# Sliding-window attention and an MLP on one core: half of the first layer as a Strassen product, and a new order of the second layer's products

## The chip, the cores and the metric

The kernel runs on one core of a Trainium2 chip. The metric is the device time of one execution in microseconds (us). The engines are named as the profile names them: PE (TensorE, matrix products), PEld (its weight loads), DVE (VectorE), ACT (ScalarE), POOL (GpSimd) and SP (SyncE, which here only issues DMAs). SBUF is the on-chip memory, PSUM the memory into which PE accumulates, in banks of 128 partitions by 512 float32.

## The reference

Four batches of 768 tokens, eight heads of 64. Each query sees itself, the 127 keys before it and the first four keys; the heads' outputs side by side are `x` (512 wide), which goes through a norm and a two-layer MLP with a residual.

```python
scores = scale * np.matmul(q, k.transpose(0, 1, 3, 2))
keep = is_sink | in_window
scores = np.where(keep, scores, -1000000000.0)
...
a = a / (np.sum(a, axis=-1, keepdims=True) + 1e-09)
return np.matmul(a, v).astype(np.float32)
...
xn = (x - mu) / np.sqrt(var + 1e-06) * g_ln
ch = np.maximum(xn @ w_ch1, 0.0) @ w_ch2        # 512 -> 2048 -> 512
return (x + ch).astype(np.float32)
```

## The kernel before, in words

The 3072 tokens are cut into 12 chunks of 256 (`NC = 12`), three to a batch. A chunk passes through these steps:

- `attend` and `value`: scores on PE (`sc`, L763, for the sinks L767), exponentials on ACT (`ex`, L777, L785), the mask on DVE (`mk`, L781), the product with v on PE (`av`, L800 and L805, one for each tile of 128 tokens), then on DVE the division (`x`, L818 and L820), the statistics (L824, L826), on POOL the root (`rs`, L832 and L833), and on DVE the normed tile (`xc`, L835). From the third chunk on, SP transposes it by DMA into `xnt` (L845), four slices of 128 model dimensions by 256 tokens.
- the first layer (`mlp`): eight blocks `u` of 256 hidden units. Each block `ph` is 8 matmuls with 256 moving columns (L880; in the first two chunks 16 with 128 columns, L873), and one ACT instruction (`rl`, L890) applies the relu and moves the bank into `hq` in bf16. `hq` is two buffers of four blocks each.
- the second layer (`wino`, from the third chunk on): a product of 256 tokens, 2048 hidden units and 512 outputs, done as seven block products p1 to p7 (Strassen's scheme in Winograd's form), 8 matmuls of 256 columns each (L960). DVE makes four sums of blocks of `hq` for each half g of the hidden units (s1 to s4, L943, eight instructions of 128x512 in a chunk). Products that several outputs share stay in one half bank and are added to while it goes on: DVE reads it in between, adding `x`, into a kept sum `tm` (`keep`, L974), and a later read adds a kept sum to another product and writes the output quarter `ot` (`final`, L981). There are four of each in a chunk. The differences of the second weights (`w2t`) are made once.

The order of the work is planned when the program is built. Every step is an `op` with an engine, a cost and a priority; a list scheduler (`Plan.run`) goes through them, and its order on each engine is the program's order. From priority 40 on PE's order is by priority alone. A chunk takes 16 units of priority: `T = 16 c + 8` in `mlp`, and `at(c, step) = 16 c - 8 + PAR[step]` for attention. So the PE order of a chunk before is: first layer u0, u1, `av` of the next chunk's first tile, u2, `av` of its second tile, u3 to u7, then p1, p2, first half of the scores of the chunk after next, p7, p6, p4, second half of the scores, p5, p3. An engine does its instructions in order, so that one that waits holds up all behind it.

Buffers come from rings. Two pairs of PSUM banks (`pair`) hold scores and attention outputs; four single banks (`one`) hold everything else, one for each block `ph` and three for a chunk's products p1 to p7 (`x`, `y`, `w`). Rings in SBUF that the change touches: `nat` 8 (q and k as loaded), `pe` 12 (exponentials), `x` 16, `xc` 6. `hq` has 8 buffers, two to a chunk.

Of the kernel before, what the change touches and what calls it, by code (L numbers as in the profile page):

```python
# [197 lines left out]
def pe(us):  # L198
    return {"PE": (us, us + Plan.PE_DRAIN)}
# [12 lines left out]
def fix(occ, extra=0.09):  # L212
    return (occ, occ + extra)
# [16 lines left out]
           w1p=(0.15, 1.7, 2.05, 2.8), pm=2, w2p=(4.5, 4.51, 4.52, 4.53), by_tile=2, wino=2, vp=(0.0, 0.1, 2.0, 2.1, 4.2, 4.3), ld1=0.05)  # L230
# [131 lines left out]
def kernel(  # L362
# [12 lines left out]
    nc = tc.nc  # L375
# [34 lines left out]
    ring("pe", 12, [128, 2, 512], BF16)  # L410
    ring("ps", 3, [128, 256], BF16)
    ring("kts", 2, [128, HP, 32], BF16)
    ring("x", 16, [128, DM], BF16)
    ring("xc", 6, [128, DM], BF16)
# [121 lines left out]
    def at(c, step):  # L536
        return 16.0 * c - 8.0 + PAR[step]
# [200 lines left out]
    def attend(c):  # L738
        b, R = c // RC, c % RC
        kq = kq_b[c]  # L740
        kprev = kq_b[c - 1] if R else None
        n = 512 if R else 384
        ps, pp_s = (Buf(f"ps{c}", "ps"), Buf(f"pss{c}", "one")) if R else (None, None)
        pes = []
        for half in range(2):
            d = at(c, "sc1" if half else "sc")
            pps = [Buf(f"s{c}{2 * half + i}", "pair") for i in range(2)]
            pbs = [Buf(f"p{c}{2 * half + i}", "pe") for i in range(2)]

            def sc(e, pps=pps, half=half):  # L750
                if R:
                    parts = [(kprev, 128, 0, 128, 0), (kq, 0, 0, 256, 128), (kq, 128, 128, 256, 384)]
                    cut = [((0, 64), (0, 128)), ((0, 192), (64, 256)), ((0, 128), (64, 128))]
                else:
                    parts = [(kq, 0, 0, 256, 0), (kq, 128, 128, 256, 256)]
                for j, pp in enumerate(pps):
                    hp = 2 * half + j
                    for i, (kt, k0, q0, q1, col) in enumerate(parts):
                        for m in range(2 if R else 1):
                            n0, n1 = (cut[i][m] if R else (0, q1 - q0))  # L760
                            for h2 in range(2):
                                rs, ks = slice(64 * h2, 64 * h2 + 64), slice(64 * m, 64 * m + 64) if R else slice(0, 128)
                                nc.tensor.matmul(pp.t[ks, h2, col + n0:col + n1], lhsT=kt.t[rs, hp, 0, k0 + ks.start:k0 + ks.stop],  # L763
                                                 rhs=kq.t[rs, hp, 1, q0 + n0:q0 + n1], start=i == 0, stop=True, skip_group_check=True)
                if R and half == 0:
                    for hp in range(HP):
                        nc.tensor.matmul(pp_s.t[32 * hp:32 * hp + 32, 0:256], lhsT=kts_b[b].t[:, hp, :],  # L767
                                         rhs=kq.t[:, hp, 1, :], start=True, stop=True, skip_group_check=True)
            sinks = R and half == 0
            scores[c] = P.op(f"sc{c}{half}", pe(2 * (384 if R else n) / 2400 + (0.21 if sinks else 0)), d, sc,  # L770
                 reads=[kq] + ([kprev] if R else [])
                 + ([kts_b[b]] if sinks else []), writes=pps + ([pp_s] if sinks else []),
                 hold=pbs + ([ps] if sinks else []), mode=("q", "c") if sinks else "q" if R else "r")
            for j, pp in enumerate(pps):
                hp = 2 * half + j
                pb = pbs[j]
                P.op(f"ex{c}{hp}", {"ACT": act(2 * n)}, d + 0.1 + 0.05 * j, lambda e, pp=pp, pb=pb: nc.scalar.activation(  # L777
                    pb.t[:, :, 0:n], pp.t[:, :, 0:n], AF.Exp, scale=scale), reads=[pp], writes=[pb])
                mm = (mask if R else mask0).rearrange("p a b c -> p a (b c)")
                P.op(f"mk{c}{hp}", {"DVE": dve(2 * n, 0.52)}, d + 0.2 + 0.05 * j, lambda e, pb=pb, mm=mm:  # L780
                     V.tensor_mul(pb.t[:, :, 0:n], pb.t[:, :, 0:n], mm),  # L781
                     reads=[Bc["mask" if R else "mask0"]], rw=[pb])
                pes.append(pb)
            if sinks:
                P.op(f"sx{c}", {"ACT": act(256)}, d + 0.6, lambda e: nc.scalar.activation(  # L785
                    ps.t, pp_s.t[:, 0:256], AF.Exp, scale=scale), reads=[pp_s], writes=[ps])
        for i in range(2):
            def part(h, n, i=i):
                col = 256 * i + 128 * n if R else 128 * (i + n)
                return pes[h // 2].t[:, h % 2, col:col + 128]  # L790
            value(c, i, pes, ps, (PAR["av2"] if c == 2 else at(c, "av")) + PAR["avi"] * i, part, [2 * c + i - 1, 2 * c + i] if R or i else [2 * c])

    def value(c, i, pes, ps, d, part, srcs):
# [24 lines left out]
        P.op(f"rc{t}", {"DVE": fix(0.115)}, d + 0.1, lambda e: V.reciprocal(rc(), pv()[:, :, :, 64]),  # L818
             reads=[po], writes=[rcb])
        P.op(f"x{t}", {"DVE": dve(512)}, d + 0.11, lambda e: V.tensor_tensor(  # L820
# [3 lines left out]
        P.op(f"bn{t}", {"DVE": fix(0.60)}, d + 0.12, lambda e: V.bn_stats(st.t[:, 8:14], x.t),  # L824
             reads=[x], writes=[st, mv])
        P.op(f"ag{t}", {"DVE": fix(0.09)}, d + 0.13, lambda e: V.bn_aggr(st.t[:, 14:16], st.t[:, 8:14]),  # L826
# [4 lines left out]
        roots[t] = P.op(f"rs{t}", {"POOL": (0.83, 0.88)}, d + (0.5 if scaled else 5), lambda e: (  # L831
# [3 lines left out]
        P.op(f"xc{t}", {"DVE": fix(0.26)}, d + (0.6 if scaled else 0.14), lambda e: V.tensor_scalar(  # L835
# [24 lines left out]

    def mlp(c):
# [5 lines left out]
        for u in range(NH1 // 2):  # L867
# [15 lines left out]
            pr = T + u + 0.5  # L883
# [12 lines left out]
        if c >= PAR["wino"]:  # L896
            return wino(c, T, hq, h1)
# [29 lines left out]
    def wino(c, T, hq, h1):  # L927
# [3 lines left out]
        deps = {n: [h1[4 * g + (0 if n[2] == "1" else 1)::2][:2] for g in range(2)] for n in part}  # L931
# [7 lines left out]
        for i, (n, x0, x1, op) in enumerate((("s3", "a11", "a21", ALU.subtract), ("s1", "a21", "a22", ALU.add),  # L939
                                             ("s2", "s1", "a11", ALU.subtract), ("s4", "a12", "s2", ALU.subtract))):  # L940
            for g in range(2):
                sb[n, g] = Buf(f"{n}_{c}{g}", "hs")
                P.op(f"{n}_{c}{g}", {"DVE": dve(512, 0.52)}, T - 4 + 4 * g + 0.2 * i, lambda e, n=n, x0=x0, x1=x1, g=g, op=op: V.tensor_tensor(  # L943
# [3 lines left out]
        reg = {"z": ("x", 0), "l2": ("y", 0), "l1": ("w", 0), "r1": ("y", 256)}  # L947
# [22 lines left out]

        def keep(name, r, done, half, pr):
            tm[name] = Buf(f"tm{name}{c}", "tm")
            i, sl = half // 2, slice(256 * (half % 2), 256 * (half % 2) + 256)
            return P.op(f"tm{name}_{c}", {"DVE": dve(256, 1.14)}, pr, lambda e: V.tensor_tensor(  # L974
                tm[name].t, at(r), xs[i].t[:, sl], op=ALU.add), reads=[done, xs[i]], hold=[bank[reg[r][0]]], writes=[tm[name]])
        oo = {}

        def final(r, done, name, half, pr):
            i, sl = half // 2, slice(256 * (half % 2), 256 * (half % 2) + 256)
            oo[half] = Buf(f"oo{c}{half}")  # L980
            return P.op(f"o{c}_{half}", {"DVE": dve(256, 1.14)}, pr, lambda e: V.tensor_tensor(  # L981
# [19 lines left out]
        last_sum[:] = [ots[0], oo[1]]  # L1001
        for half in (0, 2, 3, 1) if c == NC - 1 else (0, 1) if c in PAR["split"] else ():
            t, sl = 2 * c + half // 2, slice(256 * (half % 2), 256 * (half % 2) + 256)
            b, r = t // RB, t % RB
            P.op(f"st{t}{half}", {"SP": (0.35, 0.4)}, 3000.0 + half % 2 if c == NC - 1 else u(6), lambda e, i=half // 2, b=b, r=r, sl=sl: nc.sync.dma_start(
                out[b, 128 * r:128 * (r + 1), sl], ots[i].t[:, sl]), reads=[oo[half]], hold=[ots[half // 2]], dma=HW_S)
        for i in () if c == NC - 1 else (1,) if c in PAR["split"] else (1, 0):
            t = 2 * c + i
            b, r = t // RB, t % RB
            P.op(f"st{t}", {"SP": (0.35, 0.4)}, u(5 if i else 6), lambda e, i=i, b=b, r=r: nc.sync.dma_start(  # L1010
# [22 lines left out]
    for c in range(NC):  # L1033
        mlp(c)
# [8 lines left out]
    def guard(e):  # L1043
# [12 lines left out]
        late.t[0:1, 0:1], lhsT=last_sum[0].t[:, 511:512], rhs=ones_f, start=True, stop=True),  # L1056
# [72 lines left out]
```

## Time and profile before

| what | value |
|---|---|
| median of 3 runs | 211.26 us (210.96 to 211.36) |
| profiled execution, its own time | 211.71 us |
| span in its trace, first to last instruction | 210.2 us |
| granted clock | 1.000 |
| DVE busy, of that 85.76 to 193.75 us | 162.2 us, 87.08 of 107.99 |
| ACT busy, of that 85.76 to 193.75 us | 114.1 us, 56.10 of 107.99 |
| POOL busy, of that 85.76 to 193.75 us | 83.5 us, 33.17 of 107.99 |

The span is what lies between the first and the last instruction in the trace; the execution's own time is 1.5 us more. A busy time is the union of an engine's instructions. The stretch from 85.76 to 193.75 us begins with the first layer of the fifth chunk and ends with that of the twelfth. That is seven periods from one chunk's u0 to the next one's: 15.60, 15.20 and 15.88 us in turn, since a batch's first chunk needs less attention, and 14.63 us for the last, 15.43 us on average.

### The profile page before, as it was taken

Reading aid. Unit: us, or ns where it says so; the run is one execution under the profiler, and the core shown is the slowest. Engines: PE = TensorE matmul, PEld = TensorE weight load, DVE = VectorE, ACT = ScalarE, POOL = GpSimd, SP = SyncE. Lnnn points to the kernel's source line nnn. Section 1 sums busy time; section 2 is a strip of 40 time slices with the busy share of each in tenths; the row PEclk is TensorE's granted clock in tenths of the full one; section 3 lists DMA queues with packets and bytes.
Section 4 is the critical chain, followed back from the end, with each engine's and each line's share of the span. In section 5 each row is a group of like instructions: output and inputs, shape, how many; then the busy total and the mean of one; then the engine's idle time right before and its main releaser. Section 6 shows DMA issues by size and latency. Waiting matters only on the chain.

```text
span 210.2 us, 6259 instructions
## 1 busy us (share of the span) xinstructions
PE 203.0 (97%) x2539; PEld 167.9 (80%) x2544; DVE 162.2 (77%) x410; ACT 114.1 (54%) x168; POOL 83.5 (40%) x126
## 2 busy tenths in 40 slices
PE   6978999999999999999999999999999999999994
PEld 2657997764787997997987987987988988988883
DVE  5579759999688688798687797797787786797353
ACT  2559479837564564564556555554457457450620
POOL 7967583369058057058066066066020020020000
PEclk9999999999999999999999999999999999999999
DMA  5999999999999949939959939939954520220202
GB/s 115 156 198 191 199 191 208 189 173 154 212 167 127 172 109 136 188 78 120 166 122 150 174 79 156 172 77 151 177 100 53 150 53 3 100 50 4 103 30 83
DMA packets 101243, 27.51 MB, mean 131 GB/s; under 512 B 89556, under 2 KB 99032, under 8 KB 101208
## 3 DMA queue, kind: packets, MB, share of 16 engines
q0 software_dynamic: 67712, 13.37, 77.7%
q1 hardware_dynamic: 33208, 13.41, 35.5%
q8 instruction: 21, 0.34, 0.7%
q10 hardware_dynamic: 288, 0.26, 0.4%
q14 instruction: 14, 0.11, 0.2%
HBM read 27.30 MB, written 6.29 MB: 160 GB/s over the span
## 4 chain that ended last, share of the span: by engine, by line
PE 90%; DMA 3%; DVE 3%; POOL 2%; issue 0%; DVEq 0%
PE one L880 33%; PE one L960 30%; PE one L873 7%; PE one L911 7%; PE pair L805 5%; PE pair L763 4%; DMA n4b<-in_q_dram 3%; PE pair L800 2%; PE one L645 1%; POOL nat L599 1%; PE one L767 1%; DVE xnt L857 1%; DVE kq L568 1%; POOL vn L562 0%; DVE st L824 0%
## 5 line engine op out<-in xcount | busy, mean ns | idle before, releaser
L890 ACT ACTIVATE hq<-one 128x512 bf16<-128x512 f32 x92 | 55.0, 597 | 55.7 <-PE one L880 46.7
L880 PE MATMUL one<-xnt,w 128*128 128x256 bf16 x640 | 74.5, 273 | 0.0
L880 PEld LDWEIGHTS <-w 128*128 128x128 bf16 x640 | 61.4, 98 | 7.0
L777 ACT ACTIVATE pe<-pair 128x1024 bf16<-128x1024 f32 (+1 forms) x40 | 36.2, 960 | 23.2 <-PE pair L763 19.0
L832 POOL TENSOR_SCALAR st<-st 128x1 f32<-128x1 f32 x24 | 6.2, 259 | 88.2 <-DVE rec L818 74.6
L960 PEld LDWEIGHTS <-hs 128*128 128x128 bf16 x320 | 30.0, 98 | 5.2 <-DVE tm L974 0.3
L974 DVE TENSOR_TENSOR tm<-one,x 128x256 f32<-128x256 f32 x40 | 16.9, 422 | 12.3 <-PE one L960 12.3
L781 DVE TENSOR_TENSOR pe<-pe,mask 128x1024 bf16<-128x1024 bf16 (+1 forms) x40 | 24.9, 644 | 1.0 <-ACT pe L777 0.8
L960 PEld LDWEIGHTS <-hq 128*128 128x128 bf16 x240 | 23.5, 98 | 2.7
L562 POOL DMA_DIRECT2D vn<-in_v_dram x24 | 21.8, 922 | 2.0 <-DMA w<-in_moe_w_ch_dram 1.1
L943 DVE TENSOR_TENSOR hs<-hq 128x512 bf16<-128x512 bf16 x40 | 15.4, 413 | 5.3 <-ACT hq L890 5.2
L960 PE MATMUL one<-w,hq 128*128 128x256 bf16 x160 | 19.1, 273 | 0.0
L981 DVE TENSOR_TENSOR ot<-one,tm 128x256 f32<-128x256 f32 x40 | 16.7, 418 | 1.1 <-PE one L960 0.9
L820 DVE TENSOR_TENSOR x<-pair,rec 128x512 bf16<-128x512 f32 x24 | 16.6, 691 | 0.8
L824 DVE BATCH_NORM_STATS2 st<-x 128x6 f32<-128x512 bf16 x24 | 16.6, 692 | 0.5
L873 PE MATMUL one<-xnt,w 128*128 128x128 bf16 x256 | 16.3, 219 | 0.5 <-DVE xnt L857 0.5
L873 PEld LDWEIGHTS <-w 128*128 128x128 bf16 x256 | 14.7, 98 | 1.6 <-issue 0.5
L659 POOL DMA_DIRECT2D nat<-in_k_dram x16 | 15.0, 938 | 2.5 <-DMA w<-in_moe_w_ch_dram 2.5
L659 POOL DMA_DIRECT2D nat<-in_q_dram x16 | 14.2, 898 | 3.4 <-DMA w<-in_moe_w_ch_dram 3.4
L833 POOL TENSOR_TENSOR st<-st,mhalf 128x1 f32<-128x1 f32 x24 | 14.2, 592 | 2.0
L911 PE MATMUL one<-w,hq 128*128 128x512 bf16 x60 | 14.8, 380 | 0.2
L805 PE MATMUL pair<-vn,pe 128*128 128x65 bf16 x352 | 14.6, 193 | 0.0
(113 smaller groups left out, 245.1 us busy)
## 6 DMA issues: line engine op xcount, KB each, us to landing
out_dram<-ot SPq DMA_DIRECT2D x17, 256.0 KB
w<-in_moe_w_ch_dram POOLq DMA_DIRECT2D x8, 512.0 KB, 12.6
vn<-in_v_dram POOLq DMA_DIRECT2D x24, 128.0 KB, 7.2
nat<-in_k_dram POOLq DMA_DIRECT2D x17, 128.0 KB, 4.8
nat<-in_q_dram POOLq DMA_DIRECT2D x17, 128.0 KB, 5.3
out_dram<-ot SPq DMA_DIRECT2D x14, 128.0 KB
kq<-nat SPq DMA_TRANSPOSE x32
xnt<-xc SPq DMA_TRANSPOSE x20
```

Of the source, the lines that this page charges most:

```text
L562: P.op(f"vld{t}", {"POOL": (0.87, 0.9)}, prio, lambda e: G.dma_start(bv.t[:, :, 0:64], v[b, :, 128 * r:128 * (r + 1), :].rearrange("h p d ...
L659: lambda e, nat=nat, ap=ap: G.dma_start(nat.t, ap), writes=[nat], dma=SW, after=behind(c))
L777: P.op(f"ex{c}{hp}", {"ACT": act(2 * n)}, d + 0.1 + 0.05 * j, lambda e, pp=pp, pb=pb: nc.scalar.activation(pb.t[:, :, 0:n], pp.t[:, :, 0:n ...
L781: V.tensor_mul(pb.t[:, :, 0:n], pb.t[:, :, 0:n], mm),
L805: nc.tensor.matmul(po.t[:, h // 4, 65 * (h % 4):65 * (h % 4) + 65], lhsT=part(h, n), rhs=vn_b[tv].t[:, h, :], start=(not R and h % 4 == 0 ...
L873: nc.tensor.matmul(ph.t[:, 128 * s:128 * s + 128], lhsT=w1[u // 2][:, j, 128 * s:128 * s + 128], rhs=xnt.t[:, j, 128 * (u % 2):128 * (u % ...
L880: nc.tensor.matmul(ph.t[:, 256 * s:256 * s + 256], lhsT=w1[ht // 4][:, j, 128 * (ht % 4):128 * (ht % 4 + 1)], rhs=xnt.t[:, j, :], start=j ...
L890: nc.scalar.activation(hg.t[:, u % 4, :], ph.t, AF.Relu)
L911: nc.tensor.matmul(pc.t[:, 0:wd], lhsT=(hq[s // 2].t[:, (2 * s + i) % 4, 128 * ii:128 * ii + 128] if by_tile else hq[ht // 8].t[:, ht // 2 ...
L960: nc.tensor.matmul(at(r), lhsT=get(left, g)[:, v, s, :], rhs=rhs, start=first and n == 0, stop=n == 7, skip_group_check=True)
L974: return P.op(f"tm{name}_{c}", {"DVE": dve(256, 1.14)}, pr, lambda e: V.tensor_tensor(tm[name].t, at(r), xs[i].t[:, sl], op=ALU.add), read ...
L981: return P.op(f"o{c}_{half}", {"DVE": dve(256, 1.14)}, pr, lambda e: V.tensor_tensor(ots[i].t[:, sl], at(r), tm[name].t, op=ALU.add), read ...
```

## The change

**First layer.** From the fifth chunk on (`half=4`, so c = 4 to 11) the blocks u0 to u3 go away, and `halves` computes these 1024 hidden units in their place: as a product of 2 x 2 blocks (512 hidden units by 256 model dimensions, times 256 model dimensions by 128 tokens), again by Winograd's seven products, m1 to m7. Each is 8 matmuls with 128 moving columns. The sums of the weight blocks are made once (`weight_sums`, four DVE instructions of 128x1024 bf16, not planned before 58, 61, 64 and 67, kept in two `hq` buffers from then on). The sums of the token blocks are made for each chunk by POOL (`xt`, four of 128x256 bf16, each from two tiles in SBUF, t1 from t0 and t3 from t1). The products use three single banks, z, w and y. Bank z collects m1, then m6, then m7, then m4; y collects m5 and then m3; w holds m2. ACT copies a running bank into SBUF in float32 (`tz1` after m1, `tz5` after m5, `tz6` after m6); m6 waits for the first copy, m3 for the second, m7 for the third. DVE adds a bank and a copy into `hq` (`c11` = m2 + tz1, `c12` = y + tz6, `c22` = z + tz5), and m4 waits for `c22`. ACT then applies the relu in place (`r`, from SBUF to SBUF), and for the last block straight from the bank (`rc21`). Blocks u4 to u7 stay as they were.

**Second layer**, from the third chunk on. The products come in the order p1, p2, p6, p5, p7, p3, p4. p1, p6, p7 and p4 use one half bank one after the other, p5 and p3 another, p2 the third. There are three kept sums, three finals, and one read that writes the output directly from the last product and `x`. p6 waits for the read after p1, p7 for that after p6, p3 for that after p5, p4 for the final after p7. The priorities of s1 to s4 are new, as are the orders of the output stores.

**Order.** Attention steps of the chunks after the fifth (c > 4) have their own priorities (`h`), and so have m1 to m7 and u4 to u7 (`pos`, `pos4`). The PE order of a period becomes, for c of 4 and on: p1, p2, p6, p5 (of the chunk before), second half of the scores of the next chunk, p7, p3, m1, p4, m5, m6, `av` first tile, m2, u5, m7, m3, `av` second tile, u4, u6, m4, u7, first half of the scores of the chunk after next. Before, the first layer's first block stood behind p3; now m1 stands ahead of the last product of the chunk before.

**Rings.** `nat` 6, `pe` 10, `x` 12, `xc` 5; new are `xt` (2) and `tz` (3, float32, 128x512).

```diff
-    ring("nat", 8, [128, H, 64], BF16)
+    ring("nat", 6, [128, H, 64], BF16)
...
+    ring("xt", 2, [128, 4, 2, 128], BF16)
+    ring("tz", 3, [128, 512], FP32)
...
     def at(c, step):
-        return 16.0 * c - 8.0 + PAR[step]
+        return 16.0 * c - 8.0 + (PAR["h"] if c > PAR["half"] else PAR)[step]
...
+    def weight_sums():
...
+            P.op(f"wsum{i}", {"DVE": dve(1024, 0.52)}, PAR["wsum"] + 3.0 * i, lambda e, ap=ap, x0=x0, x1=x1, op=op, val=val:
+                 V.tensor_tensor(ap(), val(x0), val(x1), op=op), reads=...
...
+    def halves(c, T, hq):
...
+        for i, (n, x0, x1) in enumerate((("t0", "b12", "b11"), ("t2", "b22", "b12"), ("t1", "b22", "t0"), ("t3", "b21", "t1"))):
...
+            P.op(f"xt{n}_{c}", {e: dve(256, 0.52) if e == "DVE" else fix(0.65) for e in PAR["te"]}, T - PAR["tlead"] + 0.1 * i, lambda e, n=n, x0=x0, x1=x1: (V if e == "DVE" else G).tensor_tensor(
+                right(n), right(x0), right(x1), op=ALU.subtract), reads=...
...
+                for h in range(4):
+                    for kk in range(2):
+                        nc.tensor.matmul(b.t[:, 128 * h:128 * h + 128], lhsT=lt[:, kk, 128 * h:128 * h + 128], rhs=rh[:, kk, :],
+                                         start=first and h == 0 and kk == 0, stop=kk == 1, skip_group_check=True)
...
+        m1 = product(1, "z", "a11", "b11", True)
+        t1, o1 = snap(1, "z", m1)
+        m5 = product(5, "y", 0, "t0", True)
+        t5, o5 = snap(5, "y", m5)
+        m2 = product(2, "w", "a12", "b21", True)
+        total("c11", "w", m2, t1, T + pos[1] - late_)
+        m6 = product(6, "z", 1, "t1", False, [o1])
+        t2, o2 = snap(6, "z", m6)
+        m3 = product(3, "y", 3, "b22", False, [o5])
+        total("c12", "y", m3, t2, T + pos[5] - late_)
+        m7 = product(7, "z", 2, "t2", False, [o2])
+        o3 = total("c22", "z", m7, t5, T + pos[6] - late_)
+        m4 = product(4, "z", "a22", "t3", False, [o3])
...
-        for u in range(NH1 // 2):
+        strassen = c >= PAR["half"]
+        quick = halves(c, T, hq[0]) if strassen else None
+        for u in range(4 if strassen else 0, NH1 // 2):
...
-        d7 = product(2, "p7", "l2", "s3", 0, 2, True)
-        k7 = keep("t7", "l2", d7, 3, u(2) - 2)
-        d6 = product(3, "p6", "z", "s2", 0, 1, False, [k1])
-        k6 = keep("t6", "z", d6, 2, u(3) - 2)
-        d4 = product(4, "p4", "l2", "a22", 0, 3, False, [k7])
-        f2 = final("l2", d4, "t6", 2, u(4) - 1)
-        d5 = product(5, "p5", "z", "s1", 0, 0, False, [k6])
-        final("z", d5, "t7", 3, u(5) - 1)
-        keep("t5", "z", d5, 1, u(5) - 1.1)
-        d3 = product(6, "p3", "r1", "s4", 1, hi, True, [f2])
-        final("r1", d3, "t5", 1, u(6) - 0.9)
+        d6 = product(2, "p6", "z", "s2", 0, 1, False, [k1])
+        k6 = keep("t6", "z", d6, 1, u(2) - 2)
+        d5 = product(3, "p5", "l2", "s1", 0, 0, True)
+        k5 = keep("t5", "l2", d5, 3, u(3) - 2)
+        d7 = product(4, "p7", "z", "s3", 0, 2, False, [k6])
+        f3 = final("z", d7, "t5", 3, u(4) - 2)
+        d3 = product(5, "p3", "l2", "s4", 1, hi, False, [k5])
+        final("l2", d3, "t6", 1, u(5) - 1)
+        d4 = product(6, "p4", "z", "a22", 0, 3, False, [f3])
+        keep(None, "z", d4, 2, u(6) - 1)
...
     for c in range(NC):
+        if c == PAR["half"]:
+            weight_sums()
         mlp(c)
```

More of the change, by code (lines that the diff above doesn't have):

```diff
@@ L830, in value @@
         scaled = c >= PAR["wino"]
[L831 removed]
+        roots[t] = P.op(f"rs{t}", {"POOL": (0.83, 0.88)}, d + xo + (0.5 if scaled else 5), lambda e: (
             G.tensor_scalar(st.t[:, 17:18], st.t[:, 15:16], 1e-6, None, op0=ALU.add),
@@ L930, in wino @@
                 "a12": lambda g: A[g]()[:, 1, :, :, 0:128], "a22": lambda g: A[g]()[:, 1, :, :, 128:256]}
-        deps = {n: [h1[4 * g + (0 if n[2] == "1" else 1)::2][:2] for g in range(2)] for n in part}
+        if quick:
+            h1 = [None] * 4 + h1
+        deps = {n: [quick[int(n[1]) - 1] if quick and g == 0 else h1[4 * g + (0 if n[2] == "1" else 1)::2][:2] for g in range(2)] for n in part}
         sb = {}
@@ L1055 @@
     P.op("late", pe(0.06), 4000.0, lambda e: nc.tensor.matmul(
-        late.t[0:1, 0:1], lhsT=last_sum[0].t[:, 511:512], rhs=ones_f, start=True, stop=True),
+        late.t[0:1, 0:1], lhsT=last_sum[0].t[:, 255:256], rhs=ones_f, start=True, stop=True),
         reads=last_sum[1:] + [Bc["ones_f"]], hold=last_sum[0:1], writes=[late])
```

120 lines of the change are left out of this document (93 added, 27 removed).

## The prediction

> **What bounds the kernel now.** I read first the page's busy times and clock, then the chain that ended last.
>
> ```profile
> PE 203.0 (97%) x2539; PEld 167.9 (80%) x2544; DVE 162.2 (77%) x410; ACT 114.1 (54%) x168; POOL 83.5 (40%) x126
> PEclk9999999999999999999999999999999999999999
> ```
>
> ```profile
> 44.68 0.89 PE one L873 x16
> ...
> 167.28 4.37 PE one L880 x40
> 171.64 1.75 PE one L960 x16
> 173.39 0.46 PE pair L763 x22
> 173.85 0.22 PE one L767 x4
> 174.07 2.73 PE one L960 x24
> ...
> 193.75 7.09 PE one L880 x64
> 200.84 6.13 PE one L960 x56
> 206.97 0.02 issue
> 206.99 0.44 DVE ot L981
> ```
>
> The columns are start, length, engine, buffer, line and count. From 54.69 us to 206.97 us the chain is PE alone, each piece beginning where the last ended. So a microsecond taken from PE in a chunk is a microsecond of the time, as long as nothing makes PE wait. The third view, busy time by stretch (seven periods), and the groups tell how near the others are:
>
> ```profile
> 85.76:193.75 107.99, 107.99 (x1312) 93.81 (x1310) 87.08 (x217) 56.10 (x84) 33.17 (x52) 1.00 0.99 111
> ```
>
> ```profile
> L974 DVE TENSOR_TENSOR tm<-one,x 128x256 f32<-128x256 f32 x40 | 16.9, 422 | 12.3 <-PE one L960 12.3
> L820 DVE TENSOR_TENSOR x<-pair,rec 128x512 bf16<-128x512 f32 x24 | 16.6, 691 | 0.8
> L1039 ACT ACTIVATE w<-w,gt 128x512 bf16<-128x512 bf16 x11 | 7.3, 750 | 0.0
> ```
>
> The stretch's columns are PE, PEld, DVE, ACT, POOL. DVE has (107.99 - 87.08) / 7 = 2.99 us free in a period of 15.43 us; ACT 7.4 us, POOL 10.7 us.
>
> **PE's work.** Removed in each of eight chunks: four blocks, 32 matmuls of 256 columns. The chain has 40 in 4.37 us, 109.3 ns each: 3.50 us. Added: 7 x 8 = 56 matmuls of 128 columns. Line 873 is this form, each with its own weight load from the same tiles: 16 in 0.89 us, 55.6 ns each, so 3.11 us. Saved: 0.38 us a chunk, 3.05 us in eight. The second layer keeps its 56 matmuls.
>
> The rule that speaks against this: the Trainium skill, "TensorE: Matmul & The Clock Gate", section "Back-to-back issue gap", says that in a stream of weight load and matmul both set the pace, and gives 81 ns for 128 columns. By that figure 56 would take 4.54 us and the change would cost 8.3 us, an estimate; the row of line 873, with as many loads as matmuls, shows 55.6 ns, and I go by it.
>
> **DVE's work.** Added in a chunk: three sums of a bank and a copy, 128x512 into bf16. The nearest row is L820 at 0.69 us (L919, with float32 out, 0.74): 0.70 each, 2.10 us. Removed: one kept sum, 0.42 us by L974, but such reads follow each other every 0.34 us: -0.34. Net +1.76 us in a period that shrinks to 15.05 us. Of 2.99 us free, 2.99 - 0.38 - 1.76 = 0.85 us stay, so DVE goes from 81% to 94%. The weight sums, four at 0.68 us (L781, same size), come once, 2.7 us, in a stretch before 85.76 us where DVE has 6.7 of 31.8 us free: nothing, unless they land in front of a read that PE waits for (at most 0.7 us). The third and fourth chunks only lose a kept sum.
>
> **ACT's work.** Seven new instructions for four removed: three copies and one relu from a bank at 0.60 (L890), three relus from SBUF at 0.75 (L1039), less 4 x 0.60: +2.25 us, 8.0 to 10.3 of 15.05 us. Hidden under PE; without that cover 0.6 us for each copy that an m product waits for.
>
> **POOL's work.** Four sums of 128x256 from two SBUF tiles. No row shows one. Below: 0.22 us (L832, one element). Above: L833 takes 0.57 us for one element, and 128 elements cost L460 0.07 us more than one costs L832; twice 256 elements add 0.28, so 0.85. I take 0.65, 2.6 us a chunk, since a sum is more than L832's single element and lighter than L833's power. What hides them: before, the second `av` ends at 151.40 and its transposes are through at 156.94 us, 5.5 us later. In the new order PE has from there u4, u6, m4, u7, scores, p1, p2, p6, p5, scores, p7, p3 to do ahead of m1: 9.4 us. So m1 has 3.9 us to spare, and m6, which needs the third sum, 5.6 us against 0.7 to 2.6 us. SP's and POOL's queues get no further DMAs. The q and k transposes move ahead on SP, past output stores: before, those behind the loads of 124.20 us are through at 135.96 and their scores run at 142.59, 6.6 us later; the scores move up by two products, 1.75 us. Covered, and `nat` holds four buffers at a time by these rows, so six do. `hq` has six left where two chunks in flight need four.
>
> **The new waits on PE.** PE's queue is in order: what stands behind a waiting product waits too. A release costs 0.21 us from PE to the reader (the block that ends at 194.62 is read at 194.83) and 0.06 us back (DVE ends at 207.41, PE starts at 207.47).
> - m6 after the copy of m1: 0.21 + 0.60 + 0.06 = 0.87, with p4 and m5 between, 1.31. m7 after the third copy: the same 0.87 behind at most 0.4 of the second copy, with m2 and u5 between, 1.31. m4 after c22: 0.21 + 0.70 + 0.06 against m3, `av`, u4, u6, 2.7 or more. All covered, if ACT or DVE is not late by over 0.04 to 1.7 us: the exponentials of the second scores (two in 1.94 us, from 0.21 after them) end 2.15 us after these, m1 2.2 us after them.
> - p7 after the read of p6, p3 after that of p5, p4 after the final of p7: 0.69 us each against 1.33, 1.33 and 1.32. Covered.
> - p6 after the read of p1: 0.69 against p2 alone, 0.87. Before, p7 lay between as well. Here DVE may start 0.18 us late and no more. It is busy 94% of the time with instructions 0.34 to 0.72 us apart, in order; one that is in hand leaves 0.2 us on average, so this wait shows for about 0.08 us on average, 0 at best and 0.5 at worst. Eight times: 0.65 us, which I take, bounds 0 and 4.
>
> In the last chunk no attention fills PE: u7's relu and two sums of 0.45 us end 1.8 to 2.4 us after u7, and p6's second half comes after 2.2: at most 0.3 us, inside that.
>
> **The sum.** 211.71 (profiled execution: span 210.2 and 1.5 around it, unchanged, since the end is still one product, one DVE read and a store) - 3.05 + 0.65 = 209.3. That execution stood 0.45 above the median of the runs, so the forecast for a median is **208.85 us**, its own range 207.9 (no stall, and some 0.3 us of DVE time gained in the third and fourth chunks) to 210.1.
>
> **The rivals.**
> *DVE is full.* POOL's new sums and DVE may get in each other's way. A trace row bears on it:
>
> ```profile
> 17.71 0.85 POOL L833 TENSOR_TENSOR st<-st,mhalf 128x1 f32<-128x1 f32 x1
> ```
>
> ```profile
> 17.44 0.68 DVE L720 TENSOR_TENSOR pe<-pe,mask 128x1024 bf16<-128x1024 bf16 x1
> ```
>
> The POOL instruction takes 0.57 us elsewhere; here it ran 0.28 longer, while DVE worked on two SBUF tiles. No DVE row is stretched (L943, 80 of them, 0.39 to 0.43 us), but POOL never held two large tiles. The Trainium skill, "SBUF — State Buffer", section "Who interferes with whom", has this as a rule: a DVE instruction with two SBUF inputs and a GpSimd instruction that reads SBUF exclude each other, and the later one waits for the whole of the first. The POOL row agrees; that DVE waits too, no row here shows.
> As a mechanism of this kernel: DVE's instructions on two SBUF tiles are eight of L943 (0.36 apart) and four of L781 (0.60), 5.3 of 15.05 us. If half of POOL's four sums meet one and hold it half their 0.65 us, DVE loses 0.65 us a chunk: still under the 0.85 free, the forecast. At 0.85 to 1.23 us DVE fills the period and eats the gain: (14.2 + 1.1 - 15.43) x 8 = -1.0, **210.2 us**, chance 0.14.
> *The other side: slower.* The same lock at its full price, in the stretch from m1 to p6 where reads, masks and s1 to s4 crowd: each POOL sum puts DVE back by most of its length. It decides from 1.23 us a chunk, where DVE's 14.2 + 1.23 us equal the old period. At 1.6 us (four times 0.4): (14.2 + 1.6 - 15.43) x 8 = +3.0, **214.2 us**; at the full 2.6 us, 222. Or the same from thin waits: 0.38 us of stall a chunk undoes the gain. For it: DVE at 94% in front of in-order waits. Against: the unstretched rows. Chance 0.21.
> *Weight loads set the pace.* At 98 ns, the mean of a load, 56 take 5.49 us: +16 us, 227 us. Line 873's rate excludes it; 0.01.
> *The change doesn't lighten PE*, because the new priorities make PE wait elsewhere for banks (m's three and a block take all four): about the time before, 211.3 us; 0.04.
>
> **The numbers.** Forecast 0.60. Below 0.2% (0.42 us, what a measurement of this kernel can tell from no change), that is under 210.84: 0.60 and most of the second case, 0.70. Within it: part of the second and the fourth, 0.08. Slower: 0.22. For 8 in 10 the range goes to 207.7 below, and above into the slower case as far as 212.8.
>
> **What would show it.** Right: PE's chain still unbroken, 56 matmuls at 55 to 56 ns, periods near 15.1 us, idle time of PE in front of p6 under 0.1 us a chunk, DVE at 93 to 95%. Wrong: idle time of PE that DVE ends, at p6, p4 or m4; rows of L943 or L781 longer than 0.43 or 0.69 us beside POOL's sums; ACT ending waits of m6 or m7; m1 waiting for `xnt`.

## The result, and the profile after

| | before | after |
|---|---|---|
| time, median of the runs | 211.31 us (210.96 to 211.44) | 219.91 us (219.38 to 221.17) |
| ratio | 1 | 1.0418, interval 1.0371 to 1.0466 |
| span of the profiled execution | 210.2 us | 219.6 us |
| first block of the fourth chunk | 69.89 us | 73.52 us |
| seven periods of the chunks that change | 107.99 us | 113.96 us |

The forecast was 208.85 us, with 207.7 to 212.8 as its range. The kernel became 8.6 us slower. The profiled execution of after took 221.17 us, 1.3 above the median; its granted clock was 0.992 over the whole span, against 1.000, 1.000 and 0.998 in the other three. Of the 9.4 us between the spans, 3.6 are lost before the first block of the fourth chunk and 6.0 in the seven periods, which in after are counted from m1 to m1; the rest, 0.2 less, lies between and behind these stretches.

The busy row, the clock row and the chain's shares from the page of after:

```profile
PE 203.6 (93%) x2731; PEld 168.8 (77%) x2736; DVE 177.4 (81%) x430; ACT 124.5 (57%) x190; POOL 110.2 (50%) x158
PEclk9999999999996999999999999999999999999999
...
PE 56%; DMA 16%; DVE 14%; POOL 10%; issue 2%; ACT 1%; SPq 0%; DVEq 0%; POOLq 0%
PE one L1059 16%; PE one L977 11%; DMA xnt<-xc 10%; PE one L908 8%; PE one L970 6%; PE one L1008 6%; POOL xt L892 5%; PE pair L808 4%; DMA n4b<-in_q_dram 3%; DVE hq L930 3%; DMA kq<-nat 2%; DVE st L828 2%; DVE hs L1042 2%; PE pair L766 2%; DVE xc L839 2%
```

The chain that was PE alone now runs through transposes of `xnt` and POOL's sums. The view of waits (engine, what it fills, line, what released it; us in total, times, longest) says where PE stands:

```profile
POOL xt L892 <- DMA xnt<-xc: 21.7, 8, 4.6
POOL nat L662 <- DMA kq<-nat: 20.9, 7, 9.3
...
PE one L908 <- DMA xnt<-xc: 3.7, 4, 1.6
PE one L908 <- POOL xt L892: 2.9, 4, 1.0
PE one L1059 <- DVE tm L1078: 2.3, 1, 2.3
```

L908 is an m product, L892 POOL's sums, L1059 a p product, L662 a load into `nat`.

**The first loss.** POOL's timeline of after (start, length, line, and in brackets the idle time before with its releaser), then PE's:

```profile
59.62 1.75 POOL L662 DMA_DIRECT2D nat<-in_q_dram  x2 [9.33 <-DMA kq<-nat]
61.44 0.22 POOL L836 TENSOR_SCALAR st<-st 128x1 f32<-128x1 f32 x1
```

```profile
66.76 1.69 PE L1059 MATMUL one<-n4c,hs 128*128 128x256 bf16 x8 [2.31 <-DVE tm L1078]
68.24 1.91 PE L1059 MATMUL one<-n4b,hs 128*128 128x256 bf16 x8
```

With six buffers in `nat`, POOL stood 9.33 us before two q loads until transposes had emptied buffers; the root of the fourth chunk (L836) stood behind them in POOL's queue, `xc` behind the root, DVE's reads behind `xc`, and p6 on PE behind a read: 2.31 us. After it eight matmuls take 1.5 to 1.7 us in place of 0.87, for 3.4 us in which the trace shows a granted clock of 0.50: the 6 in the clock row. This slow stretch costs 1.7 us, and by the clocks above the other three executions of after had little or none of it.

**The second loss.** The timeline of after around one m1 and m6 (SPq is SP's queue):

```profile
115.51 1.86 POOL L662 DMA_DIRECT2D nat<-in_k_dram  x2
115.74 0.83 DVE L839 TENSOR_SCALAR xc<-x,st 128x512 bf16<-128x512 bf16 x1
...
116.60 1.19 SPq L554 DMA_TRANSPOSE xnt<-xc  x1
...
117.35 1.78 POOL L565 DMA_DIRECT2D vn<-in_v_dram  x2
...
121.93 0.62 PE L908 MATMUL one<-xnt,w 128*128 128x128 bf16 x8 [1.63 <-DMA xnt<-xc]
...
122.02 1.29 POOL L892 TENSOR_TENSOR xt<-xnt 128x256 bf16<-128x256 bf16 x2 [2.90 <-DMA xnt<-xc]
```

The transpose's issue ends at 117.79, but its last semaphore comes at 121.88 us, beside POOL's loads; m1 waits 1.63 us for it, and POOL's sums, which m5 and m6 need, begin only then. By the spacing of PE's matmuls, nine such gaps at m1 and m6 make 8.1 us in the sixth to tenth chunk.

### The profile page after: what moved, and what is told of

Its sections match the earlier page's. It is cut to its first block, busy times and chain, and to the rows that moved or that the text cites. A ratio compares the mean times of both kernels' runs of the same rounds, so it can differ in the third digit from the quotient of the medians.

```text
span 219.6 us, 6704 instructions
## 1 busy us (share of the span) xinstructions
PE 203.6 (93%) x2731; PEld 168.8 (77%) x2736; DVE 177.4 (81%) x430; ACT 124.5 (57%) x190; POOL 110.2 (50%) x158
## 4 chain that ended last, share of the span: by engine, by line
PE 56%; DMA 16%; DVE 14%; POOL 10%; issue 2%; ACT 1%; SPq 0%; DVEq 0%; POOLq 0%
PE one L1059 16%; PE one L977 11%; DMA xnt<-xc 10%; PE one L908 8%; PE one L970 6%; PE one L1008 6%; POOL xt L892 5%; PE pair L808 4%; DMA n4b<-in_q_dram 3%; DVE hq L930 3%; DMA kq<-nat 2%; DVE st L828 2%; DVE hs L1042 2%; PE pair L766 2%; DVE xc L839 2%
## 5 line engine op out<-in xcount | busy, mean ns | idle before, releaser
L977 PE MATMUL one<-xnt,w 128*128 128x256 bf16 x384 | 46.8, 273 | 0.0
L987 ACT ACTIVATE hq<-one 128x512 bf16<-128x512 f32 x58 | 34.5, 594 | 21.1 <-PE one L977 12.0
L977 PEld LDWEIGHTS <-w 128*128 128x128 bf16 x384 | 36.1, 98 | 3.9
L1059 PEld LDWEIGHTS <-hs 128*128 128x128 bf16 x320 | 31.5, 100 | 8.1 <-issue 2.6
L784 DVE TENSOR_TENSOR pe<-pe,mask 128x1024 bf16<-128x1024 bf16 (+1 forms) x40 | 27.5, 717 | 1.3 <-ACT pe L780 1.2
L919 ACT COPY tz<-one 128x512 f32<-128x512 f32 x24 | 13.8, 586 | 23.9 <-PE one L908 21.0
L662 POOL DMA_DIRECT2D nat<-in_q_dram x16 | 14.3, 897 | 25.0 <-DMA kq<-nat 20.9
L1059 PEld LDWEIGHTS <-hq 128*128 128x128 bf16 x240 | 22.6, 98 | 3.3 <-issue 0.3
L836 POOL TENSOR_SCALAR st<-st 128x1 f32<-128x1 f32 x24 | 6.9, 287 | 35.2 <-DVE rec L822 20.3
L892 POOL TENSOR_TENSOR xt<-xnt 128x256 bf16<-128x256 bf16 x16 | 13.2, 842 | 21.7 <-DMA xnt<-xc 21.7
L933 ACT ACTIVATE hq<-hq 128x512 bf16<-128x512 bf16 x24 | 14.9, 630 | 11.1 <-DVE hq L930 11.1
L1059 PE MATMUL one<-w,hq 128*128 128x256 bf16 x160 | 19.2, 273 | 0.0
L908 PEld LDWEIGHTS <-hq 128*128 128x128 bf16 x256 | 15.8, 98 | 4.0 <-issue 3.6
L930 DVE TENSOR_TENSOR hq<-one,tz 128x512 bf16<-128x512 f32 x24 | 15.8, 688 | 3.5 <-PE one L908 3.3
L908 PE MATMUL one<-xt,hq 128*128 128x128 bf16 x192 | 14.1, 219 | 3.0 <-POOL xt L892 2.9
L662 POOL DMA_DIRECT2D nat<-in_k_dram x16 | 14.9, 929 | 2.5 <-DMA w<-in_moe_w_ch_dram 2.5
```

Source lines behind the costliest of these rows:

```text
L662: lambda e, nat=nat, ap=ap: G.dma_start(nat.t, ap), writes=[nat], dma=SW, after=behind(c))
L892: P.op(f"xt{n}_{c}", {e: dve(256, 0.52) if e == "DVE" else fix(0.65) for e in PAR["te"]}, T - PAR["tlead"] + 0.1 * i, lambda e, n=n, x0=x0 ...
L908: nc.tensor.matmul(b.t[:, 128 * h:128 * h + 128], lhsT=lt[:, kk, 128 * h:128 * h + 128], rhs=rh[:, kk, :], start=first and h == 0 and kk = ...
L930: o = P.op(f"c{n}_{c}", {"DVE": dve(512, 1.14)}, pr, lambda e: V.tensor_tensor(block(n), banks_[bank].t.rearrange("p (i t) -> p i t", i=4) ...
L977: nc.tensor.matmul(ph.t[:, 256 * s:256 * s + 256], lhsT=w1[ht // 4][:, j, 128 * (ht % 4):128 * (ht % 4 + 1)], rhs=xnt.t[:, j, :], start=j ...
L987: nc.scalar.activation(hg.t[:, u % 4, :], ph.t, AF.Relu)
```

## The experiments

Theories: **A**, the loss is waiting for late results of DMA (buffers of `nat`, then the second tile of `xnt`). **B**, the smaller rings cost nothing. **D or F**, DVE is full, or stretched by POOL's sums. **C** and **G**, the order itself. **E**, POOL's sums are all of it. Each ratio is against the kernel before, run on the same chip.

**Parts of the change alone.** `rings_cut` is the kernel before with the four smaller rings; `nat_only`, run last, cuts one of them.

```diff
-    ring("nat", 8, [128, H, 64], BF16)
+    ring("nat", 6, [128, H, 64], BF16)
```

> The kernel before with only the four smaller rings (nat 6, pe 10, x 12, xc 5); the planned order of PE, DVE, ACT and SP is the same. Theory A (short nat ring: POOL stands waiting for q's buffers until the transposes of the chunk before have read them, and the root instructions behind it are late): PE idles some 2 us near 60 us and runs slowly after it, 213 to 216 us. Theory B (the whole loss comes from the Strassen chunks, DVE and POOL in each other's way): no change, 211.3 us.

> The kernel before with nat 6 in place of 8 and nothing else; in rings_cut with all four rings smaller (213.41 us) PE had three gaps of 1.8 us in all near 66 us. Theory A (the nat ring alone does it: POOL stands before the q loads until the chunk's transposes have freed buffers, and the root behind it is late): 212.8 to 213.6 us. Rival (another ring): 211.3 us.

Measured: 213.41 us, 1.0113 (1.0089 to 1.0137), and 213.06 us, 1.0084 (1.0067 to 1.0101). One ring does nearly all of it, by the same stand of POOL, here in the timeline of `nat_only`:

```profile
58.96 1.76 POOL L659 DMA_DIRECT2D nat<-in_q_dram  x2 [9.28 <-DMA kq<-nat]
60.79 0.22 POOL L832 TENSOR_SCALAR st<-st 128x1 f32<-128x1 f32 x1
```

`order_only` is the changed kernel with no chunk's first layer as a Strassen product and the old rings, so only the second layer's new order is left:

```diff
-           ... half=4, ...
+           ... half=99, ...
```

> The changed kernel without the Strassen half (from no chunk on) and with the old rings: only the new order of the second layer and its reads. Theory A: 211 us, plus or minus 0.5, a read less in each of ten chunks hides under PE. Theory C (the thin wait of p6 for the read after p1, with p2 alone between, costs): 0.1 to 0.5 us in each of ten chunks, 212 to 216 us, with PE idle ahead of p6.

Measured: 211.68 us, 1.0019 (1.0003 to 1.0035), 0.2 us above the range of A and below that of C. The second layer's new order with one kept sum less neither costs nor brings 1 us. The new order of attention has no run of its own.

**The nat ring given back.** `nat8`, the base of what follows, is the changed kernel with two rings changed; the order on PE, DVE, ACT and SP stays.

```diff
-    ring("nat", 6, [128, H, 64], BF16)
+    ring("nat", 8, [128, H, 64], BF16)
...
-    ring("x", 12, [128, DM], BF16)
+    ring("x", 11, [128, DM], BF16)
```

> The changed kernel with nat back at 8 (x at 11 to make room); PE, DVE, ACT and SP keep their order, only POOL's loads move. Theory A: the 2.3 us of idle PE near 64 us and the slow stretch behind it go, 219.9 - 3.7 = 216.2 us; the waits in front of m1 and m6 from the sixth to the ninth chunk stay. Theory B: 219.9 us as before.

Measured: 217.58 us, 1.0309 (1.0272 to 1.0347): 2.3 us back, and the stall near 66 us gone. The 3.7 us that were expected counted the slow stretch behind the stall too, which the other executions of after hardly had, and the gaps of the sixth to tenth chunk grew from 8.1 to 8.9 us. Its waits:

```profile
PE one L908 <- POOL xt L892: 3.7, 4, 1.5
PE one L908 <- DMA xnt<-xc: 3.5, 4, 1.9
```

**The loads put behind the transposes.** `loads_later` plans a chunk's q, k and v loads behind the transposes of `xnt` and not behind the root:

```diff
-        return [roots[2 * (c - 3) + 1]] if c >= PAR["behind"] else []
+        return [landed[2 * (c - 3) + 1]] if c >= PAR["behind"] else []
```

> As nat8, and the q, k and v loads of a later chunk wait for the transposes of xnt instead of for the root before them, so that the two don't run at the same time. Theory A (xnt is late because its transposes share the DMA engines with those loads, 4.2 to 5.3 us from xc to landing against 2.4 without loads): the second tile's transposes land 2.4 to 2.8 us after xc, PE hardly waits for xnt, what is left is POOL's sums ahead of m6; 210 to 213 us. Theory B: as nat8, 216 to 220 us, since neither DVE's nor POOL's work changes.

Measured: 217.64 us, 1.031 (1.0267 to 1.0353). A miss: the second tile lands sooner, 2.4 to 4.0 us after `xc` (3.9 to 5.3 in after), and the waits for it go, but as many others come. The loads now run beside the next chunk's first tile, which lands 3.2 to 4.7 us after its `xc` in the sixth to tenth chunk (2.4 to 2.7 in after): the tile that has loads beside it is the late one. PE's waits there:

```profile
PE pair L766 <- DMA kq<-nat: 2.7, 3, 1.2
PE one L908 <- POOL xt L892: 2.0, 2, 1.0
```

Loads that come later make the scores (L766) wait for their own transposes.

**One cause taken out at a time.** In `old_tiles` the m products and POOL's sums read the chunk before's tiles; the planner still sees the old dependences, so every engine keeps its order.

```diff
+        old = xnt_b[c - 1]
...
-        B = {...: (lambda i=i, o=128 * (j ^ f): xnt.t[:, 2 * i:2 * i + 2, o:o + 128]) ...}
+        B = {...: (lambda i=i, o=128 * (j ^ f): old.t[:, 2 * i:2 * i + 2, o:o + 128]) ...}
```

> Base: the changed kernel with eight buffers for nat and eleven for x (217.58 us, PE idle some 9.3 us in the chunks that use the seven products). Here those products and POOL's sums read the transposed tiles of the chunk before (so the output is not the reference's); the number and the order of the instructions on every engine stay. Theory A (the loss is the wait for this chunk's transposed tiles, directly in m1 and through POOL's sums in m6): the waits at m1 and m6 go, and with them about 9 us: 208.0 to 209.5 us. Rival D (the loss sits in DVE, stretched by POOL's sums, and the waits at m1 and m6 only show it first): the masks still take 0.81 us, PE waits for DVE's reads instead, 212 us or more.

Measured: 218.5 us, 1.031 (1.0252 to 1.0368). Theory A missed by 9 us, and rival D had put what came: over 212 us, with PE waiting for DVE's reads. But the edit was no clean one: freed of the wait, POOL's sums fell beside DVE's `hs` sums. So this run alone does not tell A from D. DVE's timeline there, POOL's, and PE's waits:

```profile
115.42 2.28 DVE L1043 TENSOR_TENSOR hs<-hq,hs 128x512 bf16<-128x512 bf16 x2
```

```profile
114.45 1.54 POOL L893 TENSOR_TENSOR xt<-xnt 128x256 bf16<-128x256 bf16 x2
115.95 1.47 POOL L893 TENSOR_TENSOR xt<-xnt,xt 128x256 bf16<-128x256 bf16 x2
```

```profile
PE one L1060 <- DVE tm L1079: 4.5, 5, 1.5
PE pair L766 <- DMA kq<-nat: 2.0, 2, 1.6
...
PE one L1060 <- DVE ot L1086: 1.6, 3, 0.8
```

Two `hs` sums of 0.42 us take 2.28. PE then waits 6.1 us for DVE's reads and 2.0 us for the scores' transposes, and not at all at m1 or m6.

`sums_short` keeps the tiles and shortens POOL's sums from the seventh chunk on:

```diff
-                right(n), right(x0), right(x1), op=ALU.subtract), ...
+                *(right(x)[:, :, 0:128 if c < 6 else 8] for x in (n, x0, x1)), op=ALU.subtract), ...
```

> Same base, 217.58 us. From the seventh chunk on each of POOL's four sums covers 8 columns of 128 (the output is not the reference's), so that POOL is busy some 0.2 us a sum and not 0.85; orders unchanged, m1 still waits for its own chunk's transposed tiles. Theory A (first the late tiles, POOL's sums behind them): the waits at m6 behind POOL go (1.71 + 1.11 + 0.81 + 0.50 us and part of others) and the waits at m1 stay: 213 to 215.5 us. Rival E (POOL's sums are the whole loss, through m6 and through the stretch of DVE's masks from 0.68 to 0.81 us, which delays xc): 208 to 210 us. If the sums cost nothing: 217.5 us.

Measured: 215.78 us, 1.0231 (1.0165 to 1.0297). The waits for POOL fall from 3.7 to 0.3 us, the masks back to 0.69 us; the waits for `xnt` stay, and 1.3 us for the scores' transposes come new:

```profile
PE one L908 <- DMA xnt<-xc: 3.9, 4, 1.5
...
PE pair L766 <- DMA kq<-nat: 1.3, 2, 0.8
...
PE one L908 <- POOL xt L892: 0.3, 1, 0.3
```

The time is 0.3 us above A's range. E, the sums as the whole loss, falls.

`sums_dve` changes one word of `nat8`, `te=("DVE",)`:

> Same base, 217.58 us. The four sums of a chunk go to DVE (about 0.28 us each by the halved 0.42 us rows of hs, so 1.1 us of DVE a chunk) and POOL has none. Theory A: the sums come sooner behind the tiles and DVE's masks go back to 0.68 us, but the wait for the tiles stays and DVE gets fuller: 213 to 216 us. Rival E (POOL is the whole loss): 209 to 211 us. Rival F (DVE is the limit): 218 us or more.

Measured: 231.73 us, 1.0951 (1.0911 to 1.0991), in rival F's range (218 us or more) and far from the others. But it is not that DVE has too much work, as F says: DVE stands 12.0 us before sums that wait for a late tile, and the reads behind them in its order, for which PE waits, come late too. The waits of DVE and of PE:

```profile
DVE xt L892 <- DMA xnt<-xc: 12.0, 7, 3.0
```

```profile
PE one L1059 <- DVE ot L1085: 10.1, 7, 2.0
```

**All causes out together.** `old_short` joins `old_tiles` and `sums_short`; `old_all` also lets the scores, from the sixth chunk on, read the q and k tiles of the chunk before.

```diff
+        kuse = kq_b[c - 1] if c > 4 else kq
...
-                    parts = [(kprev, 128, 0, 128, 0), (kq, 0, 0, 256, 128), (kq, 128, 128, 256, 384)]
+                    parts = [(kprev, 128, 0, 128, 0), (kuse, 0, 0, 256, 128), (kuse, 128, 128, 256, 384)]
```

> Same base (nat 8, x 11; 217.58 us), orders unchanged. Both edits together: the seven products and POOL's sums read the transposed tiles of the chunk before, and from the seventh chunk on each sum covers 8 columns (the output is not the reference's). Each alone gave little (218.5 and 215.78 us): with the tiles of the chunk before, POOL's sums fell beside DVE's `hs` sums, which took 1.14 us each in place of 0.42. Theory A+D (two causes in a row, the late tiles and POOL's sums that hold DVE's bf16 operations up; either one alone leaves the other): without both, no waits at m1 and m6, masks 0.69 and hs 0.42 us, 208.3 to 210 us. Rival G (the order itself leaves too little room in DVE, lock or not): PE still waits for DVE's reads, 212 us or more.

> old_short (214.51 us, profiled span 212.1 us) with one more edit: from the sixth chunk on the scores read the q and k tiles of the chunk before, so that they no longer wait for transposes of the own chunk (three such waits of PE stood in old_short, 1.16 + 0.68 + 2.00 us). The output is not the reference's; orders unchanged. Theory A (three late DMA results one behind the other, nothing else): 209 to 211.5 us, PE's waits in the chunks with seven products below 1.5 us in all. Rival G (something else then takes their place, DVE first of all): 213 us or more.

Measured: 214.51 us, 1.0166 (1.0117 to 1.0215), a miss, since a third wait appeared; then 210.15 us, 0.9942 (0.9925 to 0.996), as A had it. The longest line of waits that was left in the chunks of `old_short`, and PE, PEld, DVE, ACT and POOL over 64 us of before, after and `old_all` (three views):

```profile
PE pair L766 <- DMA kq<-nat: 3.3, 3, 1.8
```

```profile
100.00:164.00 64.00, 64.00 (x794) 55.45 (x792) 51.44 (x127) 35.50 (x53) 22.76 (x34) 1.00 1.27 129
```

```profile
100.00:164.00 64.00, 58.28 (x802) 50.62 (x800) 52.74 (x126) 36.74 (x59) 38.76 (x53) 1.00 1.39 131
```

```profile
100.00:164.00 64.00, 63.60 (x923) 56.46 (x921) 57.84 (x138) 41.62 (x66) 32.31 (x55) 1.00 1.40 137
```

PE idles 5.7 of 64 us in after and 0.4 in `old_all`, with the order on PE, DVE, ACT and SP unchanged and POOL's sums shorter. `old_all` is 1.2 us faster than before and its trace still has 1.57 us of gaps (around the m1 of the sixth chunk, whose sums are whole, and in the last two chunks): 2.8 us together, an estimate, against the 3.05 us forecast for PE. So the saving is there, and waiting ate it.

**More lead by order, with the right output.** The due times of the chunks with the seven products were worked out anew, with POOL's sums at 0.85 us, against transposes as late as in the traces. `lead_a` and `lead_c` let m1 and m2 take the chunk's first tile. The edit of `lead_b`, cut to what matters (`av` and `avi` are the due times of a chunk's two value products, `pos` those of m1 to m7):

```diff
-HW_X = (1.0, -0.2, 0.6)
+HW_X = (1.0, 0.8, 0.6)
...
-           h=dict(av=2.23, avi=2.88, ..., tr=-12.51, ..., xo=-0.34), ..., pos=(-1.56, 2.55, 4.2, 7.78, 0.82, 1.92, 4.09), ...
+           h=dict(av=0.01, avi=5.44, ..., tr=-20.43, ..., xo=-5.58), ..., pos=(-2.8, 1.13, 4.28, 7.66, -0.05, 0.77, 5.39), ...
...
-            P.op(f"xt{n}_{c}", {e: dve(256, 0.52) if e == "DVE" else fix(0.65) for e in PAR["te"]}, ...
+            P.op(f"xt{n}_{c}", {e: dve(256, 0.52) if e == "DVE" else fix(0.85) for e in PAR["te"]}, ...
```

> The changed kernel (nat 8, x 11, the right output) with new due times for chunks 6 to 12: the order was worked out with POOL's sums at 0.85 us and judged with transposes that land as late beside POOL's loads as the traces show (second tile 4.2 to 5.3 us after xc). m1 and m2 take the chunk's first tile and the others follow. Theory A+D (the loss is lead, and can be had by order): 209 to 211.5 us, waits for xnt below 2 us in all. Rival G (DVE beside POOL's sums is full whatever the order): 213 us or more.

> The same as the run before with m1 on the chunk's second tile as in the changed kernel, every transpose planned 1 us later, and another set of due times (second av 0.34 us later by its due time, scores' transposes 8 us earlier, m1 1.2 us earlier): Theory A+D: 209 to 212 us. Rival G: 213 us or more.

> The same with m1 and m2 on the first tile and both av groups of a chunk early (due 1.8 and 3.95 us before their old times), so that the second xc and with it the second transpose come sooner. Theory A+D: 209 to 212 us, the earliest second tile of the three. Rival G: 213 us or more.

Measured: 211.84 us, 1.0018 (0.9988 to 1.0049); 211.38 us, 0.9993 (0.997 to 1.0016); 215.54 us, 1.019 (1.0158 to 1.0223). Two of three take some 6 us back from `nat8`, though `lead_a` is 0.3 us above its range. `lead_c`, which had the second value product earliest by due time, misses: its profiled execution, 217.97 us and so 2.4 above its median, has 3.0 us of waits for POOL and 2.7 us for the scores' transposes, and a slow stretch like the one above behind the longest of these. The same 64 us in `lead_b`:

```profile
100.00:164.00 64.00, 63.77 (x919) 56.23 (x917) 59.52 (x136) 41.36 (x65) 40.27 (x54) 1.00 1.23 136
```

DVE is at 93% and its masks at 0.90 us, longer than in `nat8` (0.81), and yet PE idles 0.2 us: the stretch by POOL is not the limit, lead is. With whole sums, the right output and only the order changed, the loss against the kernel before is gone, so D and G fall. What `lead_b` loses is 1.7 us to DVE in the last two chunks. `tail_a` and `tail_b` give these due times of their own:

```diff
-                P.op(f"{n}_{c}{g}", {"DVE": dve(512, 0.52)}, T - PAR["sp"][g] + PAR["sq"][i], ...
+                P.op(f"{n}_{c}{g}", {"DVE": dve(512, 0.52)}, T - PAR["spl" if c >= NC - 2 else "sp"][g] + PAR["sql" if c >= NC - 2 else "sq"][i], ...
```

> lead_b (211.38 us) with due times of their own for the last chunk's attention and products and for DVE's second-layer sums and reads of the last two chunks, and the check of the reciprocals (three DVE instructions, 1.5 us, in front of a read that PE waited for) planned at another place. The output is the reference's. lead_b lost 0.67 + 0.31 + 0.52 + 0.20 us there. Theory A+D: 210.3 to 211.2 us, faster than before by 0.2 to 1.0 us. Rival: the waits only move, 211.4 us.

> lead_a (211.84 us, waits of 1.2 us in three chunks for POOL's third sum) with the same kind of edit at the end. The output is the reference's. Theory A+D: 210.3 to 211.5 us; the waits for POOL's sum in the seventh to ninth chunk stay. Rival: 211.8 us or more.

> The same kernel as tail_b, once more: 210.3 to 211.2 us if its gain of about 0.5 us is real, 211.3 us or more if it was chance.

Measured: `tail_b` 210.80 us, 0.9986 (0.9968 to 1.0004), and once more 210.76 us, 0.9976 (0.9958 to 0.9995); `tail_a` 211.37 us, 0.9999 (0.9984 to 1.0015). By the medians `tail_b` is some 0.5 us faster than the kernel before in both measurements. One interval includes 1 and the other ends at 0.9995, so the gain is at the edge of what these runs can tell; of the 3.05 us forecast it is a sixth. Two more sets of due times, meant to give yet more lead, made it worse:

> tail_b (210.80 us, right output, PE waits of 0.90 us for xnt in one chunk and 0.81 us for DVE's reads) with due times worked out against transposes that land 0.2 to 1.4 us later than the traces' mean and POOL's sums of 0.66 to 0.85 us before their collisions, m1 due 1.8 us later and the second av later by 1.5. Theory A (what is left is lead): 209.5 to 210.6 us. Rival (it is the thin waits for DVE, which are moved and not lost): 210.8 to 211.5 us.

> The same search from another start: m1 as in tail_b, the second av due 0.1 us later, u blocks 0.4 to 1 us earlier. Theory A: 209.8 to 210.7 us. Rival: 210.8 to 211.5 us.

Measured: 212.1 us, 1.0044 (1.002 to 1.0068), and 215.91 us, 1.0221 (1.0202 to 1.024). In the first, small waits of 0.2 to 0.7 us stand at eight places, for DVE, POOL and `xnt`; in the second, m1 stands in four chunks, 3.3 us by PE's gaps, for `xnt` in three of them by the view of waits; that trace is of its fastest execution, 213.88 us, so what the others lost beyond it isn't shown. That the transposes land at other times than those that the due times were worked out for would explain both, but no run tests it.

## Why the prediction was wrong, step by step

- **PE's work: right.** Eight m matmuls follow in 0.445 us, 55.6 ns each, as the row of line 873 said, and `old_all` shows 2.8 of the 3.05 us.
- **"m1 has 3.9 us to spare": the step that failed, and with it the 5.6 us for m6, which rest on the same reading.** The 5.5 us from the second `av` to "transposes through" were read from the end of SP's row at 156.94, which is the end of the issue; the transpose's last semaphore came at 158.17, and that chunk had no q, k or v loads beside it any more. The trace of before had the late tile already: in the fourth to ninth chunk the second tile landed 4.4 to 5.1 us after `xc`, and in the ninth 8.7 us after the second `av` (136.47 to 145.15), which leaves 0.7 of the 3.9 us. In the chunk shown above `av` ends at 110.64, `xc` at 116.57 (5.9 us, against 4.3 in before: bank sums, `hs` sums and a read stand ahead of it on DVE, and `xc` itself takes 0.83 us in place of 0.41), the tile lands at 121.88: 11.2 us. The prediction's own 9.4 us of PE work for m1 falls 1.8 us short; the trace has 1.63.
- **"`nat` holds four buffers at a time, so six do": wrong.** Counted where loads are released by a root; near 50 us they run ahead, and six were full for 9.3 us. This is the second step that failed, a term put at nothing: `nat_only` prices it at 1.8 us in the old order, `nat8` at 2.3 in the new.
- **POOL's sums: 0.65 us taken, 0.83 measured** (0.66 alone, up to 1.15 beside DVE), inside the upper bound of 0.85 on average. The larger part of their cost is that they start late.
- **The lock between POOL and DVE: real, and smaller than in the case that was put with the forecast, 0.65 us a chunk.** In after, 9 masks of 28 began while a sum ran and took 1.0 us on average, up to 1.17, in place of 0.68: 3.0 us more in all, about 0.4 a chunk, which DVE had room for. The Trainium skill, "SBUF — State Buffer", section "Who interferes with whom", says that the later of the two waits for the whole of the first. The rows agree: masks already running when a sum begins stay at 0.68 us or less, later ones take up to 1.17. The rival that ended slower rested on this lock at 1.6 us a chunk. Its sign was right, its mechanism not: `sums_short` without the lock still stood at 215.78, `lead_b` with more of it at 211.38.
- **DVE at 93 to 95%: right** once PE is fed, 59.52 of 64 us in `lead_b`. In after it is 52.74, because DVE waits for PE.
- **p6 behind the read of p1: 0.65 us taken, less measured.** In the eight chunks of after p6 follows without a gap; its one wait, 2.31 us, is the stall in the third chunk's second layer. The small gaps of the last two chunks, 0.13 to 0.17 us, stand before p7 and p3. Where PE is fed, in `lead_b`, p6 waits 0.6 us once and 0.07 twice, so it is the right place in kind.
- **The new instructions of DVE and ACT: right or nearly so.** DVE's sums of a bank and a copy take 0.69 us (0.70 taken), ACT's copies 0.59 (0.60) and its relus from SBUF 0.63 (0.75).
- **The scores' transposes "covered": true in after, by luck.** The 135.96 us, too, are the end of an issue; the last semaphore came at 139.76, so 2.8 of the 6.6 us were there, against the 1.75 that were to be taken. With the two waits ahead of them taken out, `old_short` shows 3.3 us of waits just there.
- The range, up to 212.8 us, held stalls of DVE alone, none of DMA, though "m1 waiting for `xnt`" stood on the list of what would prove it wrong.

Not settled: which orders are safe, and how much later a transpose lands beside a given load. Time was gained and lost by due times alone, from 210.8 to 215.9 us, and what they were expected to give was wrong by as much as 5 us.

## What to carry to other kernels

A planned kernel whose bound engine is never idle has as much slack as its orders happen to leave; work taken from that engine shortens every lead in front of it, so each result that it consumes, DMA first of all, must be asked for its time from source to landing in the chunk where most traffic runs. Read the landing from the consumer or the semaphore, never from the end of the issuing queue's row, and price a smaller ring where its loads run ahead, not where they are released by something else. When one wait is removed and the time stays, remove the next one too before the theory is dropped: here it took three. And then look for a run with the right output that removes them, as `lead_b` did.

## What the runs showed of the hardware

- A DMA transpose of 128x512 bf16 lands 2.44 us after `xc` with nothing beside it, and 3.9 to 5.3 us after it (the second tiles of six chunks of after; 4.4 to 5.1 in before) while POOL's loads of q, k and v are in flight.
- After PE had stood for 2.3 us, the granted clock was 0.50 for 3.4 us in the profiled execution of after, and matmuls of 256 columns came about 0.10 us further apart, 1.7 us in all. In `lead_c` the same came behind a gap of 2.5 us; behind the gap of 2.0 us at an m1 of `nat8` it did not.
- `xc`, 0.41 us, took 0.51 to 0.83 us, 0.69 on average, in four cases of after in which POOL did nothing but issue loads. Each time it began 0.2 to 0.5 us after POOL had begun to issue a load, and ended 0.09 us after that issue's end (116.48 us in the chunk shown above, where the view has two issues in one line). In before, where it begins 0.08 us after the start of such an issue, it kept 0.41; the masks beside such issues kept 0.68 us.
